# Two linear-attention and two gated-MLP layers on one core: attention output token-major, k^T v in PSUM, shared weight slots, and a written order for every engine

## The chip, the core and the metric

The kernel runs on one core of a Trainium2 chip. The metric is the time on the device in microseconds (us); each kernel is run several times and the median is quoted. The kernel before was run again beside every set of experiments; its medians there lay between 1913.2 and 1914.6 us, so medians of different sets can be compared to about 0.1%.

The engines, as these kernels use them, are PE (matrix products), DVE (vector work), ACT (functions of one input), POOL (further vector work) and SP (issues loads and stores). Matrix products are written to PSUM, which this kernel uses as eight banks of 128x512 f32; the other tiles lie in SBUF. Each engine has its own queue of instructions, and one engine can wait for another's result: PE's waits in the changed kernel add to 89 us. DVE and POOL take their instructions in queue order.

## The reference, cut to what matters

```python
# S = 2048 tokens, D = 1024, H = 32 heads of 32, F = 3584; all bf16
def A(x, wqkv, wo):                       # x is layer-normalized
    q, k, v = (x @ wqkv) split into heads
    phi = lambda t: where(t > 0, t + 1, exp(t)) + 1e-6
    kv  = phi(k)^T v          # per head, 32 x 32, summed over all tokens
    z   = sum of phi(k) over tokens
    o   = (phi(q) kv) / (phi(q) . z + 1e-6)
    return o @ wo
def B(x, w_gate, w_up, w_down):           # x is layer-normalized
    return ((x @ w_gate) * (x @ w_up)) @ w_down
x = x + A(ln(x)); x = x + B(ln(x)); x = x + A(ln(x)); x = x + B(ln(x))
```

## The kernel before

X stays on the chip as 16 tiles of 128 tokens. Tiles are normalized, transposed on PE (`xnT`), and used in groups of 512 tokens. The parts that the change and the argument touch, with cuts marked `# ...`:

```python
def phi_from_psum(ps, dst, work):            # two ACT passes, one DVE, one POOL
    m = work.tile([P, NB], F32, tag="phi_m")
    nc.scalar.activation(out=m[:], in_=ps, func=ACT.Exp)
    r = work.tile([P, NB], F32, tag="phi_r")
    nc.scalar.activation(out=r[:], in_=ps, func=ACT.Relu)
    nc.vector.tensor_scalar(out=m[:], in0=m[:], scalar1=1.0, scalar2=1e-6, op0=ALU.min, op1=ALU.add)
    nc.gpsimd.tensor_tensor(out=dst, in0=m[:], in1=r[:], op=ALU.add)

# k^T v of one 128-token tile; v carries 128 columns of ones beside its 128 columns
for c2 in range(KD // 2):
    kp = psum.tile([P, 2, 2 * P], F32, tag="aux")
    for j in range(2):
        c = c2 * 2 + j
        nc.tensor.matmul(out=kp[:, j, :], lhsT=pk[:, c * P:(c + 1) * P], rhs=v[:, c, :], start=True, stop=True)
    # ... first tile: copy
    nc.vector.tensor_tensor(out=acc[:, c2 * 2:c2 * 2 + 2, :], in0=acc[:, c2 * 2:c2 * 2 + 2, :], in1=kp[:], op=ALU.add)

# attention output of 512 tokens, channel-major: every denominator is repeated over 32 rows
for c in range(KD):
    # ... nps = numerator matmul, dps = denominator matmul, both 128x512
    den = work.tile([P, NB], F32, tag="den")
    nc.scalar.activation(out=den[:], in_=dps[:], func=ACT.Identity, bias=eps6[:], scale=1.0)
    nc.vector.reciprocal(out=den[:], in_=den[:])
    nc.vector.tensor_tensor(out=oT[:, c, :], in0=nps[:], in1=den[:], op=ALU.mult)
# ... then oT @ wo, added to X
```

The program text names no order of execution across its parts. A scheduler takes the instructions, knows their dependences, and decides in which order each engine gets them; for instance it lets the first gate matmuls of layer B run inside the output stage of layer A.

## Time and profile before

| | |
|---|---|
| time | 1913.93 us (1913.43 to 1914.03, 3 runs) |
| PE busy | 1756 us, 92% of the span |
| large matmuls (128x512) that any version needs | 7424 |
| DVE / ACT / POOL busy | 801 / 410 / 167 us |

From the page, the span in 40 slices: tenths busy of PE and DVE, and the PE clock that was granted, in tenths.

```profile
PE   5999756799999999999999995677999999999999
...
DVE  7554699941221222222254448999211211211211
...
PEclk9999877899999999999999997788999999999999
```

Twice PE falls to 5 to 7 tenths while DVE rises to 9: these are the output stages of the two attention layers. The windows view gives this stage by stage (each line: the stretch, its length, then busy time of each engine, clock, DMA share and GB/s):

```profile
core 0: us, PE busy (x) PEld busy (x) DVE busy (x) ACT busy (x) POOL busy (x), PEclk, DMA share, GB/s
0.00:18.50 18.50, 0.30 (x4) 0.30 (x5) 11.30 (x31) 2.13 (x5) 2.49 (x8) 1.00 0.95 332
18.50:223.00 204.50, 193.19 (x1021) 96.50 (x1020) 115.97 (x216) 103.82 (x169) 81.15 (x64) 0.99 0.10 32
223.00:386.00 163.00, 102.68 (x366) 38.66 (x366) 157.81 (x148) 30.00 (x46) 0.00 (x0) 0.76 0.12 39
386.00:975.00 589.00, 586.98 (x2822) 269.81 (x2821) 141.84 (x256) 85.05 (x149) 1.53 (x2) 1.00 0.32 102
```

The lines are the start, QKV (the products with wqkv), the attention output, and layer B. In the third, DVE is busy 158 of 163 us. What it does there is in the groups view (instructions of one line of the program: busy us, mean ns of one, idle time before them):

```profile
L194 DVE RECIPROCAL den<-den 128x512 f32<-128x512 f32 x64 | 211.0, 3325 | 3.4 <-ACT den L193 3.4
```

64 reciprocals of 3.3 us: 6.5 ns per element, and 31 of 32 results are copies. Layer B, in contrast, is at PE's floor. Its timeline (start, duration, engine, instructions) shows units of eight matmuls that start 1.73 us apart, 216 ns for a matmul:

```profile
450.74 1.89 PE L231 MATMUL gp<-xnT,wg 128*128 128x512 bf16 x8
452.46 1.89 PE L235 MATMUL up<-xnT,wu 128*128 128x512 bf16 x8
```

### The profile page before, as it was taken

Reading aid. Unit: us, or ns where it says so; the run is one execution under the profiler, and the core shown is the slowest. Engines: PE = TensorE matmul, PEld = TensorE weight load, DVE = VectorE, ACT = ScalarE, POOL = GpSimd, SP = SyncE. Lnnn points to the kernel's source line nnn. Section 1 sums busy time; section 2 is a strip of 40 time slices with the busy share of each in tenths; the row PEclk is TensorE's granted clock in tenths of the full one; section 3 lists DMA queues with packets and bytes.
Section 4 is the critical chain, followed back from the end, with each engine's and each line's share of the span. In section 5 each row is a group of like instructions: output and inputs, shape, how many; then the busy total and the mean of one; then the engine's idle time right before and its main releaser. Section 6 shows DMA issues by size and latency. Waiting matters only on the chain.

```text
span 1916.1 us, 19920 instructions
## 1 busy us (share of the span) xinstructions
PE 1756.1 (92%) x8320; PEld 802.8 (42%) x8320; DVE 801.0 (42%) x1159; ACT 410.4 (21%) x689; POOL 166.8 (9%) x138
## 2 busy tenths in 40 slices
PE   5999756799999999999999995677999999999999
PEld 2444322344444444444444442233444444444444
DVE  7554699941221222222254448999211211211211
ACT  5544211211111111111134442121111111110110
POOL 2344200000000000000034441000000000000000
PEclk9999877899999999999999997788999999999999
DMA  7000210084135125122050004001840540450410
GB/s 263 1 1 1 77 56 0 1 274 143 45 97 167 45 88 164 57 88 88 1 176 1 1 1 132 0 1 52 277 135 20 163 145 22 139 169 23 132 44 23
DMA packets 145882, 158.57 MB, mean 83 GB/s; under 512 B 3456, under 2 KB 134528, under 8 KB 145792
## 3 DMA queue, kind: packets, MB, share of 16 engines
q1 hardware_dynamic: 136000, 139.47, 22.7%
q10 hardware_dynamic: 9792, 17.83, 2.7%
q8 instruction: 65, 1.06, 0.2%
q14 instruction: 25, 0.20, 0.0%
HBM read 153.09 MB, written 4.19 MB: 82 GB/s over the span
## 4 chain that ended last, share of the span: by engine, by line
PE 79%; DVE 11%; DMA 3%; issue 3%; ACT 2%; POOL 0%; ACTq 0%; POOLq 0%; DVEq 0%
PE ps L249 20%; PE gp L231 19%; PE up L235 19%; PE ps L154 11%; DVE den L194 7%; PE ps L143 4%; PE ps L201 3%; PE kp L168 1%; DVE oT L195 1%; DMA wg<-in_B_w_gate_dram 1%; DMA wd<-in_B_w_down_dram 1%; DVE X L204 1%; PE pt L101 1%; ACT xnT L102 1%; DMA X<-in_A_x_dram 1%
## 5 line engine op out<-in xcount | busy, mean ns | idle before, releaser
L231 PE MATMUL gp<-xnT,wg 128*128 128x512 bf16 x1792 | 426.0, 381 | 1.2 <-ACT gs L238 1.2
L235 PE MATMUL up<-xnT,wu 128*128 128x512 bf16 x1792 | 424.0, 379 | 0.6 <-DVE hT L239 0.6
L239 DVE TENSOR_TENSOR hT<-gs,up 128x512 bf16<-128x512 f32 x224 | 153.6, 686 | 581.5 <-PE up L235 559.9
L249 PE MATMUL ps<-wd,hT 128*128 128x512 bf16 x1792 | 391.5, 379 | 0.0
L238 ACT COPY gs<-gp 128x512 f32<-128x512 f32 x224 | 131.0, 585 | 760.6 <-PE gp L231 718.7
L231 PEld LDWEIGHTS <-wg 128*128 128x128 bf16 x1792 | 176.1, 98 | 215.6 <-issue 6.1
L235 PEld LDWEIGHTS <-wu 128*128 128x128 bf16 x1792 | 175.1, 98 | 212.6 <-issue 1.2
L249 PEld LDWEIGHTS <-hT 128*128 128x128 bf16 x1792 | 174.4, 98 | 206.5
L154 PE MATMUL ps<-wqkv,xnT 128*128 128x512 bf16 x1024 | 235.7, 381 | 1.4 <-ACT r L115 1.4
L194 DVE RECIPROCAL den<-den 128x512 f32<-128x512 f32 x64 | 211.0, 3325 | 3.4 <-ACT den L193 3.4
L201 PE MATMUL ps<-wo,oT 128*128 128x512 bf16 x512 | 150.8, 445 | 37.9 <-DVE oT L195 26.7
L252 DVE TENSOR_TENSOR X<-X,ps 128x512 bf16<-128x512 bf16 x64 | 44.0, 688 | 320.7 <-PE ps L249 320.7
L154 PEld LDWEIGHTS <-xnT 128*128 128x128 bf16 x1024 | 100.3, 98 | 107.9 <-issue 2.5
L116 DVE TENSOR_SCALAR m<-m 128x512 f32<-128x512 f32 x128 | 73.1, 571 | 125.4 <-ACT m L113 125.4
L143 PE MATMUL ps<-xnT,wqkv 128*128 128x512 bf16 x512 | 112.1, 379 | 3.8 <-ACT xnT L102 3.3
L113 ACT ACTIVATE m<-ps 128x512 f32<-128x512 f32 x128 | 76.5, 597 | 178.7 <-PE ps L154 140.3
L201 PEld LDWEIGHTS <-oT 128*128 128x128 bf16 x512 | 55.2, 109 | 131.4 <-issue 55.7
L102 ACT COPY xnT<-pt 128x1024 bf16<-128x1024 bf16 x64 | 61.1, 1021 | 225.3 <-PE pt L101 223.0
L187 PE MATMUL nps<-pqT,KVm 128*128 128x512 bf16 x64 | 33.1, 517 | 80.8 <-DVE oT L195 73.2
L117 POOL TENSOR_TENSOR pk<-m,r 128x512 bf16<-128x512 f32 x64 | 81.0, 1266 | 132.0 <-ACT r L115 129.4
L193 ACT ACTIVATE den<-dps,eps_77 128x512 f32<-128x512 f32 x64 | 43.7, 686 | 225.5 <-DVE oT L195 189.1
L117 POOL TENSOR_TENSOR pqT<-m,r 128x512 bf16<-128x512 f32 x64 | 81.2, 1269 | 109.7 <-ACT r L115 99.6
(42 smaller groups left out, 707.8 us busy)
## 6 DMA issues: line engine op xcount, KB each, us to landing
wg<-in_B_w_gate_dram SPq DMA_DIRECT2D x56, 1024.0 KB, 5.4
wu<-in_B_w_up_dram SPq DMA_DIRECT2D x56, 1024.0 KB, 7.4
wd<-in_B_w_down_dram ACTq DMA_DIRECT2D x56, 256.0 KB, 5.6
wqkv<-in_A_wqkv_dram SPq DMA_DIRECT2D x12, 1024.0 KB, 12.0
wo<-in_A_wo_dram SPq DMA_DIRECT2D x4, 1024.0 KB, 12.9
out_dram<-X SPq DMA_DIRECT2D x16, 256.0 KB, 2.0
X<-in_A_x_dram ACTq DMA_DIRECT2D x12, 256.0 KB, 6.1
X<-in_A_x_dram SPq DMA_DIRECT2D x4, 256.0 KB, 4.5
```

Of the source, the lines that this page charges most:

```text
L102: nc.scalar.copy(out=xnT[:, :, tl * P:(tl + 1) * P], in_=pt[:])
L113: nc.scalar.activation(out=m[:], in_=ps, func=ACT.Exp)
L117: nc.gpsimd.tensor_tensor(out=dst, in0=m[:], in1=r[:], op=ALU.add)
L143: nc.tensor.matmul(out=ps[:], lhsT=wqkv[:, k, c * P:(c + 1) * P], rhs=xnT[:, k, :], start=(k == 0), stop=(k == KD - 1))
L154: nc.tensor.matmul(out=ps[:], lhsT=xnT[:, k, tl * P:(tl + 1) * P], rhs=wqkv[:, k, D + n * NB:D + (n + 1) * NB], start=(k == 0), stop=(k == ...
L194: nc.vector.reciprocal(out=den[:], in_=den[:])
L201: nc.tensor.matmul(out=ps[:], lhsT=oT[:, c, tl * P:(tl + 1) * P], rhs=wo[:, c, n * NB:(n + 1) * NB], start=(c == 0), stop=(c == KD - 1))
L231: nc.tensor.matmul(out=gp[:], lhsT=wg[:, k, j * P:(j + 1) * P], rhs=xnT[:, k, :], start=(k == 0), stop=(k == KD - 1))
L235: nc.tensor.matmul(out=up[:], lhsT=wu[:, k, j * P:(j + 1) * P], rhs=xnT[:, k, :], start=(k == 0), stop=(k == KD - 1))
L238: nc.scalar.copy(out=gs[:], in_=gp[:])
L239: nc.vector.tensor_tensor(out=hT[:, f, :], in0=gs[:], in1=up[:], op=ALU.mult)
L249: nc.tensor.matmul(out=ps[:], lhsT=hT[:, f, tl * P:(tl + 1) * P], rhs=wd[:, f, n * NB:(n + 1) * NB], start=(f == 0), stop=(f == KF - 1))
```

## The change: its intent, and the diff

The intent was to take the wide reciprocals away and, with an order written by hand for every engine, to have PE never wait. The whole kernel was rewritten; its parts are:

1. Attention output token-major. KV carries four extra columns per 128 channels, one denominator for each head, so a tile needs 32 reciprocals per token and not 1024. The result must then be transposed on PE.
2. k^T v stays in three PSUM banks over all 16 tiles; 132 columns, not 256; no DVE adds. That leaves one bank for transposes instead of two.
3. phi: one ACT pass, min and add on POOL, a max on DVE that reads PSUM.
4. rstd (the layernorm's 1/sqrt of variance) as a power on POOL instead of ACT's square root and DVE's reciprocal.
5. Weights, `hT` and attention's intermediates share the same SBUF slots; SP alone issues the loads.
6. The scheduler is switched off (`manual_schedule`). Each engine gets its instructions in the order of the program text, which a helper `weave` interleaves.

```diff
+def weave(main, fill, first, step):
+    out, fill = [], list(fill)
+    for i, u in enumerate(main):
+        out.append(u)
+        if fill and i >= first and (i - first) % step == 0:
+            out.append(fill.pop(0))
+    return out + fill
 ...
+    ctx.enter_context(tc.manual_schedule())
 ...
+    def phi(ps, dst):
+        e = work.tile([P, NB], F32, tag="e", name="e")
+        nc.scalar.activation(out=e[:], in_=ps[:], func=ACT.Exp)
+        nc.gpsimd.tensor_scalar(out=e[:], in0=e[:], scalar1=1.0, scalar2=1e-6, op0=ALU.min, op1=ALU.add)
+        nc.vector.scalar_tensor_tensor(out=dst, in0=ps[:], scalar=1.0 + 1e-6, in1=e[:], op0=ALU.add, op1=ALU.max)
 ...
+    def o_unit(t):            # one tile: three PSUM banks of 3, 3 and 2 chunks of 132 columns
+        ...
+                den = small.tile([P, n, HC], F32, tag=f"den{n}", name="den")
+                nc.vector.tensor_scalar(out=den[:], in0=view[:, :, P:ZW], scalar1=1e-6, scalar2=None, op0=ALU.add)
+                nc.vector.reciprocal(out=den[:], in_=den[:])
+                nc.vector.tensor_tensor(out=onat[tl]..., in0=view[:, :, 0:P]..., in1=den[:]...to_broadcast([P, n, HC, 32]), op=ALU.mult)
 ...
+            ln_stats(0)
+            ln_stats(1)
+            do([apply_unit(0), tx(0, 0), stats_unit(2), k_unit(0, 0), apply_unit(1), tx(1, 0), stats_unit(3),
+                k_unit(1, 0), apply_unit(2), tx(2, 0), k_unit(2, 0), apply_unit(3), tx(3, 0), k_unit(3, 0)])
 ...
+        do(weave(kv_group(2), next_ln(3), 0, 1))
 ...
+        def out_group(g):
+            return [u for t in range(g * TPG, (g + 1) * TPG)
+                    for u in (out_unit(t, 0), out_unit(t, 1), stats_unit(t))]
+        do(weave(out_group(0), o_group(1) + to_group(1), 0, 1))
```

A `k_unit` is eight matmuls and a phi; `apply_unit` normalizes a tile on DVE; `tx` transposes it; `stats_unit` takes a tile's mean and variance on DVE and its rstd on POOL; `o_unit` and `to_unit` make and transpose a tile of the attention output.

## The prediction

> **What bounds it now.** PE is costed by start-to-start: in layer B's timeline eight 128x512 matmuls take 1.73 us, 216 ns each[...]. Busy time by stretch (windows view):
> - 0-18.5 us: hardly any PE work; rstd waits on ACT until 15.5 us behind twelve X loads. First real matmul: 23.6 us.
> - QKV, 18.5-223 and 975-1165: PE 94-98% busy.
> - Attention and output, 223-386 and 1165-1327: DVE 97%, PE 63% (some of it B's), clock 0.75. The bound is RECIPROCAL 128x512, 3.3 us x64 = 211 us, also in the chain of waits (7%).
> - B, 386-975 and 1327-1912: PE 100%, clock 1.00; at its floor.
>
> **What changes.** 7424 large matmuls stay: x 0.216 = 1603 us.
> - Removed: the wide reciprocals and their ACT copies; 128 numerator/denominator matmuls of 512 columns (28 us); 120 accumulate adds (75 us DVE); one of two ACT passes of phi (76 us); 17 table loads; loads and rstd on ACT.
> - Added: 256 token-major matmuls of 132 columns, 256 transposes. Transposes in layer B cost about 54 ns each (25 us windows hold 140 instead of 116 matmuls); so about 57 ns for 132 columns (estimate). All small matmuls together: about 72 us.
> - Moved: phi's min/add to POOL[...], its last op to DVE (0.69 us); both under the 1.73 us unit. rstd becomes a POOL power.
>
> PE floor: 1675 us.
>
> **Above it (estimates).**
> - Start, +17 us: one queue brings X then K weights; first K unit at 10-12 us, then four tiles each wait for transpose and ACT copy (1.02 us)[...].
> - Output stage, +12 us per A layer: an o unit costs DVE about 2.2 us (three den adds, three 12-element reciprocals of 0.15, three multiplies of 0.35-0.48), plus add 0.61 and stats 1.4 per tile. Where o and output units alternate, DVE needs 3.5 us per 2.2 us of PE: with three aux banks PE waits 1.3 us, three times in each of three groups.
> - Layer boundaries +8 us; tail and latencies +7 us.
>
> Of the gain, 140-150 us is in the attention stages, 10 at the start, 20 in QKV.
>
> **Prediction: 1730 us, range 1708 to 1768.** Faster by over 2%: 0.96; within: 0.03; slower: 0.01.
>
> **What would show each step.**
> - DVE busy falls from 801 to 560-600 us; RECIPROCAL 128x12 near 0.2 us.
> - PE clock near 1.00 except the start and perhaps o/output stretches (above 0.9).
> - A(0) from first matmul to first gate matmul falls from 365 to about 275 us; each B layer stays at 585 +- 5 us.
> - The waits list's largest PE entries: o matmul <- DVE (aux buffer), first K <- ACT copy; together 30-50 us of PE idleness.
> - If o-stage waits are near zero, I overstated DVE; then about 1705.
>
> **What would make it wrong.** POOL: its power or 128x512 op may be several times slower; over 1.7 us it would bound every Q unit (+0.5 us per phi is +60 us). Strict order on DVE: phi behind a waiting op blocks PE through four mm banks. Late weights: B's down weights load only once A's output weights are free, and gate/up loads queue behind these 7 MB; I expect 22 us against 41 us of slack.

The clock at the start: the trace of the kernel before has it at 1.00 there, from 18.5 to 50 us; in the changed kernel it was 0.50 from 20 to 40. The sum came to 1675 + 17 + 24 + 8 + 7 = 1731 us and was put as 1730. That POOL's part of phi would stay under the 1.73 us unit was the estimate; the nearest op measured on POOL was the two-input add, 1.27 us. The 17, 8 and 7 us are estimates too. What an o unit and the late weights cost was estimated from records of the kernel before: for the o unit, a 128x1 reciprocal of 0.15 us, 128x128 products 0.20 us apart and a 128x512 product followed after 0.60 us; for the late weights, 7.3 MB at the 332 GB/s of its start, 22 us.

## The result, and the profile after

The changed kernel takes 1808.21 us (median of 4 runs, 1806.58 to 1810.64), before 1913.98 us. The ratio is 0.9444 (95% interval 0.9431 to 0.9458). Ratios in this text are not quite the ratio of the medians. It is clearly faster, but by 106 us and not by 184, and above the predicted range (1708 to 1768).

The three rows of the page again:

```profile
PE   4889987999999999999989999789999999999999
...
DVE  2333368422211221122122225872211111111111
...
PEclk6999998999999999999999999899999999999999
```

The deep dips are gone, but PE now stands below 9 tenths in five of the first seven slices, and the clock is low in the first. In the groups view POOL has a new costly group, and the wide reciprocal has become a small one:

```profile
L197 POOL TENSOR_SCALAR e<-e 128x512 f32<-128x512 f32 x128 | 245.8, 1920 | 143.4 <-ACT e L196 136.4
...
L266 DVE RECIPROCAL den<-den 128x12 f32<-128x12 f32 x64 | 14.6, 228 | 2.2
```

The reciprocals cost what was expected (0.23 us). The POOL half of phi takes 1.92 us, more than the 1.27 us of the two-input add that POOL did in the kernel before, and more than the 1.73 us of the matmul unit that feeds it. By stage:

```profile
0.00:43.00 43.00, 17.95 (x64) 7.50 (x66) 9.50 (x19) 7.33 (x9) 10.94 (x31) 0.71 0.89 293
43.00:212.00 169.00, 152.67 (x852) 75.50 (x867) 56.89 (x97) 58.40 (x92) 99.62 (x71) 0.99 0.08 24
212.00:337.00 125.00, 105.04 (x627) 52.94 (x637) 91.55 (x239) 27.79 (x34) 39.28 (x45) 0.92 0.07 20
337.00:929.00 592.00, 585.34 (x2794) 270.85 (x2848) 130.90 (x213) 86.77 (x133) 13.34 (x32) 1.00 0.33 109
```

In the first 43 us PE is busy 18 and no other engine for even a third of the time. (DMA works at 0.89, but it loads ahead: only the first K unit waited for a load, 2.8 us.) In the second stretch no engine but PE is above 60%. Who made PE wait is in the waits view, here of PE alone (total us, times, longest; the four largest entries):

```profile
PE pt L172 <- DVE xn L165: 32.9, 17, 6.9
PE aux L261 <- DVE H L267: 27.8, 46, 1.3
PE ps L206 <- DVE H L198: 8.3, 4, 3.3
PE pt L172 <- ACT H L173: 6.9, 6, 1.2
```

All PE entries together are 89 us. `pt` is the PSUM bank of the transposes, `aux` the three banks of the o units, `ps` the four banks of the large matmuls. The first entry is transposes that wait for the normalized tile; the second, o units that wait for a bank.

The timeline of the start shows how the first comes about. One round of four:

```profile
20.29 3.60 PE L206 MATMUL ps<-W_74,xT_70 128*128 128x512 bf16 x8 [1.10 <-ACT xT_70 L173]
...
23.93 0.60 ACT L196 ACTIVATE e<-ps 128x512 f32<-128x512 f32 x1 [3.69 <-PE ps L206]
24.61 1.94 POOL L197 TENSOR_SCALAR e<-e 128x512 f32<-128x512 f32 x1 [4.11 <-ACT e L196]
26.59 0.69 DVE L198 SCALAR_TENSOR_TENSOR H<-ps,e 128x512 bf16<-128x512 f32 x1 [7.05 <-POOL e L197]
27.19 0.54 DVE L165 TENSOR_SCALAR xn<-X,mv,rstd 128x1024 bf16<-128x1024 bf16 x1
...
27.79 1.03 PE L172 MATMUL pt<-ident,xn 128*128 128x128 bf16 x8 [3.90 <-DVE xn L165]
28.86 1.01 ACT L173 COPY xT_70<-pt 128x1024 bf16<-128x1024 bf16 x1 [4.34 <-PE pt L172]
...
29.93 3.60 PE L206 MATMUL ps<-W_74,xT_70 128*128 128x512 bf16 x8 [1.10 <-ACT xT_70 L173]
```

The normalize step at 27.19 needs nothing from the phi at 26.59: its rstd was ready at 9.2 us. It is merely behind it in DVE's queue, because the text has `k_unit(1, 0)` ahead of `apply_unit(2)`. So each tile waits for exp, the POOL op and the max of the tile before it, and a round is 9.6 us. The clock is low in these rounds too: eight matmuls take 3.60 us, not 1.89, and the granted clock is 0.50 from 20 to 40 us, with gaps of 3.9 us ahead of the transposes. How long a gap must be for that is not shown; shorter gaps go with a low clock as well: in the first output stage it was 0.50 at 250.1-256.8, 277.4-280.7 and 301.3-308.0 us, and no gap between matmuls there was over 1.5 us.

In QKV, POOL's queue and DVE's queue hold each other. The timeline around a PE wait of 3.26 us:

```profile
129.34 0.69 DVE L198 SCALAR_TENSOR_TENSOR H<-ps,e 128x512 bf16<-128x512 f32 x1 [1.30 <-POOL e L197]
...
129.95 1.28 DVE L151 BATCH_NORM_STATS2 st<-X 128x6 f32<-128x512 bf16 x2
...
131.56 0.23 POOL L155 TENSOR_SCALAR ve<-mv 128x1 f32<-128x1 f32 x1 [2.25 <-DVE mv L153]
...
132.53 1.93 POOL L197 TENSOR_SCALAR e<-e 128x512 f32<-128x512 f32 x1
...
135.23 1.89 PE L206 MATMUL ps<-W_75,xT_72 128*128 128x512 bf16 x8 [3.26 <-DVE H L198]
```

The POOL op at 132.53 had its input (an exp that ended at 126.9 us); it stood behind the 0.23 us op of a layernorm, which waited for statistics on DVE, which stood behind a phi, which had waited for POOL.

To see how much is lost where, I take the starts of the matmul records and count what lies beyond 216 ns for 512 columns and 56 to 58 ns for 128 and 132 (in the changed kernel eight transposes start at 149.24 us, eight 132-column matmuls at 149.69 and the next unit at 150.16). Over all matmuls that the kernel issues these nominal times add to 1675 us, the predicted floor. Of the 133 us above it, about 34 lie before 43 us, 26 between 43 and 250 us, 20 and 22 in the two output stages, 13 in the second QKV and the boundary before it, and 5 in layer B; the rest is tail and spells of low clock. (After 43 us, starts that are just twice the nominal apart are left out of these numbers, since they can be a missing record as well as a halved clock.)

### The profile page after: what moved, and what is told of

It reads as the page before. It is cut to its first block, busy times and chain, and to the rows that moved or that the text cites. A ratio compares the mean times of both kernels' runs of the same rounds, so it can differ in the third digit from the quotient of the medians.

```text
span 1808.9 us, 20106 instructions
## 1 busy us (share of the span) xinstructions
PE 1707.1 (94%) x8535; PEld 804.7 (44%) x8704; DVE 527.6 (29%) x1030; ACT 341.7 (19%) x514; POOL 300.2 (17%) x280
## 4 chain that ended last, share of the span: by engine, by line
PE 83%; POOL 8%; DVE 6%; ACT 1%; issue 1%; DMA 0%; another core or an unknown queue 0%; SPq 0%; ACTq 0%
PE ps L302 43%; PE aux L314 21%; POOL e L197 8%; PE ps L206 5%; PE ps L288 5%; PE ps L216 5%; PE pt L172 2%; DVE H L267 2%; PE ps L248 1%; DVE st L151 1%; DVE X L280 1%; DVE den L266 1%; PE aux L231 1%; DVE H L198 1%; ACT e L196 1%
## 5 line engine op out<-in xcount | busy, mean ns | idle before, releaser
L306 DVE TENSOR_TENSOR H<-gs,ps 128x512 bf16<-128x512 f32 x224 | 154.0, 687 | 613.7 <-PE ps L302 610.9
L197 POOL TENSOR_SCALAR e<-e 128x512 f32<-128x512 f32 x128 | 245.8, 1920 | 143.4 <-ACT e L196 136.4
L305 ACT COPY gs<-ps 128x512 f32<-128x512 f32 x224 | 131.2, 585 | 731.4 <-PE ps L302 705.6
L314 PEld LDWEIGHTS <-H 128*128 128x128 bf16 x1792 | 174.2, 98 | 207.3
L280 DVE TENSOR_TENSOR X<-X,aux 128x512 bf16<-128x512 bf16 x64 | 44.0, 688 | 328.2 <-PE aux L314 312.2
L196 ACT ACTIVATE e<-ps 128x512 f32<-128x512 f32 x128 | 76.4, 597 | 179.9 <-PE ps L206 93.6
L198 DVE SCALAR_TENSOR_TENSOR H<-ps,e 128x512 bf16<-128x512 f32 x64 | 44.3, 692 | 193.4 <-POOL e L197 193.4
L302 PEld LDWEIGHTS <-W_75 128*128 128x128 bf16 x640 | 62.5, 98 | 75.7
L302 PEld LDWEIGHTS <-W_74 128*128 128x128 bf16 x640 | 62.4, 98 | 74.9
L302 PEld LDWEIGHTS <-W_77 128*128 128x128 bf16 x576 | 56.2, 98 | 68.1
L302 PEld LDWEIGHTS <-xT_73 128*128 128x128 bf16 x576 | 56.2, 98 | 68.1
L302 PEld LDWEIGHTS <-xT_72 128*128 128x128 bf16 x576 | 56.1, 98 | 67.1
L302 PEld LDWEIGHTS <-W_76 128*128 128x128 bf16 x576 | 56.0, 98 | 66.4
L151 DVE BATCH_NORM_STATS2 st<-X 128x6 f32<-128x512 bf16 x128 | 81.7, 680 | 3.5 <-DMA X<-in_A_x_dram 3.5
L302 PE MATMUL ps<-xT_71,W_75 128*128 128x512 bf16 x317 | 75.4, 379 | 0.3
L302 PE MATMUL ps<-xT_70,W_75 128*128 128x512 bf16 x318 | 75.5, 379 | 0.2
L288 PEld LDWEIGHTS <-H 128*128 128x128 bf16 x512 | 50.8, 103 | 55.9 <-issue 10.1
L302 PE MATMUL ps<-xT_70,xT_72 128*128 128x512 bf16 x316 | 75.4, 379 | 0.2
L302 PE MATMUL ps<-xT_70,xT_73 128*128 128x512 bf16 x312 | 74.8, 379 | 0.4
L302 PE MATMUL ps<-xT_71,W_76 128*128 128x512 bf16 x314 | 75.0, 379 | 0.3
L302 PE MATMUL ps<-xT_70,W_74 128*128 128x512 bf16 x310 | 74.8, 379 | 0.4
```

The lines of the kernel that those rows point to most:

```text
L151: nc.vector.bn_stats(out=st[:, c, :], in_=X[:, t, c * NB:(c + 1) * NB])
L196: nc.scalar.activation(out=e[:], in_=ps[:], func=ACT.Exp)
L197: nc.gpsimd.tensor_scalar(out=e[:], in0=e[:], scalar1=1.0, scalar2=1e-6, op0=ALU.min, op1=ALU.add)
L198: nc.vector.scalar_tensor_tensor(out=dst, in0=ps[:], scalar=1.0 + 1e-6, in1=e[:], op0=ALU.add, op1=ALU.max)
L280: nc.vector.tensor_tensor(out=X[:, t, n * NB:(n + 1) * NB], in0=X[:, t, n * NB:(n + 1) * NB], in1=ps[:], op=ALU.add)
L288: nc.tensor.matmul(out=ps[:], lhsT=oT[(t // TPG) % 2][:, c, tl * P:(tl + 1) * P], rhs=wo[n][:, c, :], start=(c == 0), stop=(c == KD - 1))
```

## The experiments

Theory: nothing that the change computes is too slow; the written order makes PE wait, because long chains stand ahead of independent work in the in-order queues of DVE and POOL. Rivals: the POOL op is a bound by its rate; DVE's total in the output stage is; loads and the low clock (0.50 from 20 to 40 us; the expectations call it cold) set the start; the shared slots keep layer B out of the output stage of layer A. All thirteen kernels below gave correct results; unless something else is said, each has four runs, and its edit is against the changed kernel.

### e1_start and e1b_start: the order of the start

```diff
-            do([apply_unit(0), tx(0, 0), stats_unit(2), k_unit(0, 0), apply_unit(1), tx(1, 0), stats_unit(3),
-                k_unit(1, 0), apply_unit(2), tx(2, 0), k_unit(2, 0), apply_unit(3), tx(3, 0), k_unit(3, 0)])
+            do([apply_unit(0), tx(0, 0), stats_unit(2), apply_unit(1), tx(1, 0), stats_unit(3),
+                apply_unit(2), tx(2, 0), k_unit(0, 0), apply_unit(3), tx(3, 0),
+                k_unit(1, 0), k_unit(2, 0), k_unit(3, 0)])
```

> Only the first four tiles are reordered: the four normalize steps and three of the four transposes stand ahead of the first K unit, so that no normalize step stands behind a phi on DVE's queue. In the changed kernel the four rounds start 9.6 us apart and end at 43 us. Theory (in-order DVE queue: normalize of tile t+1 waits for exp, the 1.9 us POOL op and phi of tile t): the four K units now follow one another, the fourth ends at 20 to 27 us, and the whole takes about 1790 us (18 less). Rival (loads of X and weights, or the cold PE clock, set the pace): rounds stay 7 to 10 us apart, the whole stays within 5 us of 1808.

Measured: 1792.57 us (ratio 0.937), 16 us less than the changed kernel. The one normalize step that I had left behind a phi made PE wait 3.9 us again, and the 56 matmuls from 19.77 us took 14.72 us, 263 ns each in place of 216. In e1b_start it too stands ahead of `k_unit(0, 0)`:

> As e1_start, with the fourth normalize step also ahead of the first K unit. In e1_start it alone was left behind a phi, and PE waited 3.9 us for it at 18.9 us. Theory (DVE order behind phi): that wait goes too, another 4 to 6 us off e1_start, 1786 to 1789 us in all. Rival (the rest of the start is the cold clock): the same as e1_start, 1792.

Measured: 1788.66 us (ratio 0.9343), another 3.9 us. K units follow one another from 14.0 us on. The order of DVE's queue explains 20 us at the start, part of it through the clock: the loads are as before, and 63 matmuls from 14.03 us take 15.25 us, 242 ns each, where in the changed kernel eight take 3.60, 450 ns each. What the start still loses beyond the nominal time of its matmuls is 14 us.

### e2_phi_act and e2_pool_one_op: POOL's part of phi

```diff
-        nc.scalar.activation(out=e[:], in_=ps[:], func=ACT.Exp)
-        nc.gpsimd.tensor_scalar(out=e[:], in0=e[:], scalar1=1.0, scalar2=1e-6, op0=ALU.min, op1=ALU.add)
+        nc.scalar.activation(out=e[:], in_=ps[:], func=ACT.Relu, scale=-1.0)
+        nc.scalar.activation(out=e[:], in_=e[:], func=ACT.Exp, scale=-1.0)
```

exp(-relu(-x)) is min(exp(x), 1). The 1e-6 is left out here, and one in e4_all_b.

> Phi without POOL: exp(-relu(-x)) in two ACT passes, then the same DVE max. Theory (the POOL op of 1.92 us, longer than the 1.73 us unit and in one queue with the layernorm's power, starves PE): PE gaps in QKV of the first layer (26 us between 43 and 250 us, 28 us before) fall to under 12 us and the start shortens by 5 us or more; the whole takes 1775 to 1788 us. Rival (the QKV gaps come from the DVE order of layernorm work, not from POOL): under 10 us gained, 1798 or more. If two ACT passes (1.2 us per unit) become the limit instead, ACT shows above 80% in QKV and the time does not fall.

Measured: 1773.03 us (ratio 0.9269), 35 us less, a little more than expected. POOL is out of the chain of phi, and PE's waits for phi in QKV are gone from the waits view. From the end of the fourth K unit to the first o unit, gaps between matmuls fell from 18 to 2 us, and the fourth K unit ends 6 us earlier.

The other edit keeps the op on POOL, with one step of arithmetic:

```diff
-        nc.gpsimd.tensor_scalar(out=e[:], in0=e[:], scalar1=1.0, scalar2=1e-6, op0=ALU.min, op1=ALU.add)
+        nc.gpsimd.tensor_scalar(out=e[:], in0=e[:], scalar1=1.0, scalar2=None, op0=ALU.min)
```

> POOL keeps phi's min but drops the add of 1e-6, so its op has one arithmetic step in place of two (results differ far below bf16). If the 1.92 us comes from the second arithmetic step, the op falls to 1.0 to 1.3 us and the whole to 1780 to 1795 us; if it is a cost per element whatever the steps, the op stays at 1.8 to 1.95 us and the time at 1808.

Measured: 1791.32 us (ratio 0.9365). Neither branch was right about the op: it fell to 1.49 us, not to 1.0 to 1.3.

```profile
L197 POOL TENSOR_SCALAR e<-e 128x512 f32<-128x512 f32 x128 | 190.8, 1492 | 177.8 <-ACT e L196 177.1
```

The second step of arithmetic costs 0.43 us of the 1.92. At 1.49 us the op is under the unit's 1.73, and 17 us are gained. DVE is not what slows the op: at 24.61 us in the timeline of the start it takes 1.94 us while DVE stands idle.

### e3_stats: less DVE work in the output stage

```diff
         def out_group(g):
-            return [u for t in range(g * TPG, (g + 1) * TPG)
-                    for u in (out_unit(t, 0), out_unit(t, 1), stats_unit(t))]
+            outs = [out_unit(t, n) for t in range(g * TPG, (g + 1) * TPG) for n in range(2)]
+            if g < NG - 1:
+                return outs
+            return [u for t in range(TPG) for u in (stats_unit(t), outs[t])] + outs[TPG:]
 ...
-        do(weave(out_group(3), ln0, 0, 1))
+        do(weave(out_group(3), ln0, 2, 1))
 ...     # layer B, first group: statistics of the other twelve tiles between gate/up units
+                    if g == 0 and fb * 4 + j < 3 * TPG:
+                        main.append(stats_unit(TPG + fb * 4 + j))
```

> The layernorm statistics (1.41 us of DVE per tile) of twelve tiles move from the output stage into layer B's gate/up units, where DVE is about 20% busy; those of the first four move behind the last o unit. Theory (in the output stage DVE is the bound: 4 x 2.63 for o units + 8 x 0.62 + 4 x 1.41 = 21.2 us per group against 17.4 us of PE): per group 15.5 us of DVE is below PE's 17.4, the PE gaps of the output stages (20 and 22 us) fall to 8 to 14 each and the whole to 1785 to 1796 us. Rival (the stage waits on the latency of each o unit with its three aux banks, not on DVE's total): under 6 us gained.

Measured: 1780.04 us (ratio 0.9296), 28 us less, more than expected. From the first output matmul to the first gate matmul, each output stage fell from 94 to 81 us, and the gaps in it from 24 to 12 us (the 20 and 22 above are counted over shorter stretches). So the statistics did hold this stage up, by their share of DVE's time or by their place ahead of o units in its queue; the run does not tell these apart. The waits for the aux banks only fell from 27.8 to 20.0 us in total; that the rest is the latency of an o unit (2.67 us of DVE, by the mean times of its nine instructions), as the rival has it, is likely but not shown apart. The clock in the first output stage (about 250 us to its end) rose from 0.90 to 0.99, which adds to the gain.

### e_sched: the written order undone

```diff
-    ctx.enter_context(tc.manual_schedule())
```

> The changed kernel with one line removed, so that the scheduler orders every engine's instructions again; program text, tiles and shared slots stay. Theory (a good part of the lost time comes from the written order on the in-order queues of DVE and POOL): the start shortens and the QKV gaps shrink; the whole falls to 1765 to 1795 us. Rival (the loss is in the work itself: the POOL op, the o unit's DVE cost, shared slots that keep layer B out of the output stage): the whole stays at 1800 or more.

Measured: 1714.48 us (ratio 0.8955). This one line costs 94 us, more than I had expected of it, and nothing else in the program was altered: the POOL op still takes 1.92 us (246 us busy in all), the o unit has the same DVE work, and the shared slots are there. All waits of PE in this trace:

```profile
PE pt L171 <- POOL rstd L156: 9.8, 1, 9.8
PE ps L205 <- ACT xT L172: 4.7, 4, 1.4
PE ps L215 <- DVE H L197: 4.5, 3, 1.9
PE aux L260 <- DVE H L266: 4.3, 6, 1.3
PE ps L205 <- DVE H L197: 0.3, 1, 0.3
PE aux L230 <- ACT H L218: 0.3, 1, 0.3
```

That is 24 us in place of 89. At the start DVE now has all four normalize steps ahead of the first phi:

```profile
9.18 2.47 DVE L164 TENSOR_SCALAR xn<-X,mv,rstd 128x1024 bf16<-128x1024 bf16 x4
18.21 0.69 DVE L197 SCALAR_TENSOR_TENSOR H<-ps,e 128x512 bf16<-128x512 f32 x1 [6.57 <-POOL e L196]
```

### e4_all_b: all repairs in the written order

The edits of e1b_start, e2_phi_act and e3_stats, and three small ones: the reciprocal reads the denominators in PSUM directly, o and transpose units alternate, and the transposes at layer B's end are spread.

```diff
-                nc.vector.tensor_scalar(out=den[:], in0=view[:, :, P:ZW], scalar1=1e-6, scalar2=None, op0=ALU.add)
-                nc.vector.reciprocal(out=den[:], in_=den[:])
+                nc.vector.reciprocal(out=den[:], in_=view[:, :, P:ZW])
 ...
-        do(weave(out_group(0), o_group(1) + to_group(1), 0, 1))
+        do(weave(out_group(0), o_to(1), 0, 1))      # o, o, to, o, to, o, to, to; same for 1 and 2
 ...     # end of layer B: apply of the next tile together with the transposes of this one
-                    for t in range(gg * TPG, (gg + 1) * TPG):
-                        fill += [apply_unit(t), tx(t, gg)]
+                ts = range(TPG, 3 * TPG)
+                fill = [apply_unit(TPG)] + [(lambda t=t: (tx(t, t // TPG)(), t + 1 < 3 * TPG and ln_apply(t + 1))) for t in ts]
```

> All repairs of the fixed order together: start order, phi on ACT twice and DVE (no POOL), statistics moved, denominators inverted straight from PSUM (0.6 us less DVE per o unit; the 1e-6 is far below the sums), o and transpose units spread evenly, the transposes at the end of layer B spread. If the causes add up: 1808 less 21 (start), 27 (phi; its share of the start is already counted), 22 (output stages), 5 (boundary) is 1733; range 1728 to 1750, faster than the kernel before with the attention part alone (1767). If they overlap or a new wait appears: 1760 or more.

Measured: 1710.78 us (ratio 0.8933), 97 us less than the changed kernel and better than expected. The three tested causes alone add to 83 us (20 + 35 + 28); the other three edits were not tried apart, so how far the causes overlap is open. The repaired written order is as fast as the scheduler with the unrepaired work (1714 us), but not as fast as the scheduler with the same repairs (1696 us, next).

### e5_sched_phi and e5_sched_all: the scheduler with the repairs

The edit of e2_phi_act, and all edits of e4_all_b, each without the `manual_schedule` line.

> The changed kernel with the scheduler's order and phi without POOL. In the written order this repair of phi gained 35 us. Theory (the 1.92 us POOL op hurts only through what the written order puts behind it): with the scheduler's order it gains under 10 us, 1705 to 1714. Rival (POOL's rate is a bound of its own): 20 us or more gained, 1695 or less.

Measured: 1700.91 us (ratio 0.8888). Phi without POOL gains 13.6 us here and 35 in the written order. That is between the two expectations: most of what the POOL op cost came from order, but not all of it.

> All repairs of e4_all_b, but ordered by the scheduler and not as written. If order is the common cause, the repairs and the scheduler remove the same waits: 1695 to 1714 us, a few us below the better of the two (1711 and 1714), because the POOL op and 0.6 us of DVE per o unit are gone too. If the scheduler undoes the hand-made spreading: 1715 or more.

Measured: 1695.59 us (ratio 0.8857), the fastest version, 11.4% under the kernel before. Its page:

```profile
PE   7999999999999999999999999999999999999999
...
PEclk9999999999999999999999999999999999999999
```

All 8704 matmul records are in this trace. Their nominal times add to about 1675 us; the span is 1694.3 us, of which 9.5 are before the first matmul, and from the first matmul's start to the last's it is 1681 us. Little is left to gain but the start and the work itself. The four kernels make a square: written order 1808 us and repaired 1711, scheduler 1714 and repaired 1696. The order costs 94 us with the work as it was and 15 us with the repairs, so most of the loss needed both: the order, and the long chains that it put ahead of PE's work.

### p_attn: the first part of the change alone, on the kernel before

```diff
-                    for c in range(KD):
-                        # nps, dps: 128x512; den on ACT; reciprocal 128x512; multiply
+                    for tl in range(TPG):
+                        onat = work.tile([P, D], BF16, tag="onat")
+                        for c0 in range(0, KD, 3):
+                            # n = 3, 3, 2 matmuls of 132 columns into one bank; den (+1e-6), reciprocal
+                            # and multiply as in o_unit
+                        pt = psum.tile([P, KD, P], BF16, tag="tr")
+                        # eight transposes of onat into pt
+                        nc.scalar.copy(out=oT[:, :, tl * P:(tl + 1) * P], in_=pt[:])
```

> The kernel before with one part of the change alone: token-major attention output with denominators as extra columns (masked KV with 132 columns, 12-element reciprocals, PE transposes of the output), scheduler and everything else as before. Theory (the wide reciprocal was all that bounded this stage; the fixed order adds little to it): the stage falls from 163 to about 95 to 105 us in both layers and the whole to 1780 to 1810 us, as much as the full change gave. Rival (the gain needs the fixed order and the PSUM accumulation too): 1830 us or more.

Measured: 1766.91 us (1762.09 to 1771.66, ratio 0.9227), better than expected and 41 us better than the full change. This part alone gains 147 us. The output stage that began near 223 us ends at 309.5 us, 87 us later; in the kernel before it lasted to 389.5 us. The first gate matmul of layer B comes right after it:

```profile
309.69 1.89 PE L241 MATMUL gp<-xnT,wg 128*128 128x512 bf16 x8
```

This also bears on the rival of the shared slots. They are not shared here and layer B does not start inside the output stage; in e_sched they are shared, and the first gate matmul follows the last output matmul by the same 0.2 us (282.2 after 282.0). So the slots cost no overlap that another version had made use of, except the kernel before, whose output stage was idle enough to let it in. And e5_sched_all, which has the shared slots, lies only about 20 us above PE's floor.

### b_manual: the written order alone, on the kernel before

```diff
+    ctx.enter_context(tc.manual_schedule())
```

> The kernel before with its program text as it is, but executed in the written order. Theory (a written order costs wherever work with long chains stands ahead of independent work in one in-order queue): clearly slower than 1914, 1960 to 2100 us. Rival (only the weave of the changed kernel is at fault): within 1% of 1914.

Measured: 2171.77 us (2 runs, ratio 1.1345), even slower than expected: the text of this kernel was never meant to be an order. Its largest PE wait is 111 us, numerator matmuls waiting for the multiply of an earlier chunk.

### p_kv and p_kv2: k^T v in PSUM, on top of p_attn

```diff
-                acc = p1.tile([P, KD, 2 * P], F32, tag="acc")
+                        if t == 0:
+                            acc = [psum.tile([P, NB], F32, tag="aux", bufs=3, name="acc") for _ in range(3)]
+                        # eight matmuls of 132 columns accumulate into acc over all tiles; no DVE adds
 ...     # banks of PSUM: mm 4, tr 2, aux 2  ->  p_kv: mm 4, tr 1, aux 3;  p_kv2: mm 3, tr 2, aux 3
```

> The kernel before with two parts of the change: the token-major attention output (as in p_attn, 1767 us) and k^T v kept in PSUM over all tiles, 132 columns wide; scheduler, phi and weight loads as before. The three accumulator banks leave one bank for transposes instead of two. Estimate: 256 matmuls of 132 instead of 256 columns, 109 - 57 ns each, 13 us less on PE; the 75 us of DVE adds were off the chain: 1750 to 1758 us. If the single transpose bank costs more than that gains: 1767 or more.

Measured: 1790.59 us (ratio 0.9351), 24 us slower than p_attn; the estimate was wrong, and the other branch came true. The waits view of p_attn has this line for transposes that wait until ACT has copied an earlier tile out of the transpose bank:

```profile
PE pt L103 <- ACT xnT L104: 3.4, 11, 0.7
```

and in p_kv it has become

```profile
PE pt L103 <- ACT xnT L104: 21.6, 21, 1.9
```

This kernel transposes the four tiles of a group one after the other. With one bank each waits for the 1.01 us copy of the one before. p_kv2 gives the second bank back and takes one from the matmuls:

> p_kv with two transpose banks and three matmul banks in place of one and four. Theory (the single transpose bank makes PE wait for each ACT copy at every group boundary, 21.6 us of waits against 3.4 in p_attn): those waits fall below 6 us and the time to 1750 to 1772 us. Rival (the accumulators themselves, or the order that the scheduler makes of them, cost it): the time stays above 1780. If three matmul banks bind instead, PE waits for phi (ACT or DVE) appear in the QKV stage.

Measured: 1759.44 us (ratio 0.9189). The wait is 3.9 us, and the accumulation in PSUM now gains 7 us over p_attn by the medians, where 13 were estimated. This is uncertain by several us, since the runs of p_attn spread over 9.6 us; the two profiled executions differ by 12.5 us. The bank was the cost, not the accumulators. Three matmul banks bind little: PE's waits for phi's ACT pass are 2.6 us, after 1.0 in p_attn.

## Why the prediction was wrong, point by point

The direction was right. The time was not: 1808 us is 40 us above the upper end.

What held:

- The bound before. p_attn removes the wide reciprocal, keeps the scheduler, and gains 147 us: within the 140 to 150 that the prediction gave to the attention stages. The changed kernel itself did not get all of it.
- The PE floor of 1675 us. The nominal times of the matmuls add to it again, which only repeats the sum; but e5_sched_all takes 1681 us from its first matmul to its last.
- Layer B at 585 +- 5 us each, nearly: from its first matmul to its last the first takes 593 us (337.1 to 930.6, with the transposes at its end), which is just outside, and the second 585 (1219.8 to 1805.1). The loads of shared slots cost no visible wait.
- A 12-element reciprocal near 0.2 us: 0.23. DVE busy fell further than said, to 528 us and not 560 to 600.

The step that failed is "Above it (estimates)": 55 us were allowed for what PE loses, and 133 were lost.

| term | predicted | measured | what the runs showed |
|---|---|---|---|
| start | 17 | about 34 | the normalize step of each tile stood behind the phi of the tile before (e1b_start: 20 us; the 14 left are within the 17) |
| output stages | 2 x 12 | 20 and 22 of gaps | an o unit keeps DVE 2.67 us, not 2.2; statistics on top of it and a clock of 0.90 (e3_stats: 28 us) |
| QKV, boundaries, tail, latencies | 15 | 39 in the two QKV stretches, and 5 in B | the POOL op in one queue with the layernorm's small ops (e2_phi_act: 35 us, a part of it at the start) |

Two sentences of the prediction are at the root. The first is "both under the 1.73 us unit", of phi's parts on POOL and DVE. For POOL that was the author's estimate and not measured; the op took 1.92 us. The prediction's own warning ("+0.5 us per phi is +60 us") would make about 24 us of the 0.19 us over the unit; without POOL 35 us were gained in the written order (e2_phi_act) and 13.6 in the scheduler's (e5_sched_phi). The second is the whole treatment of the written order: the prediction named "Strict order on DVE: phi behind a waiting op blocks PE" among what could go wrong, and costed it at nothing. It was in the text of the program to be read, `k_unit(1, 0)` ahead of `apply_unit(2)`. What the order costs is measured: 94 us (e_sched), of the 133 that the time lies above PE's floor. Without them, at 1714 us, the time would have stood inside the range.

The checks that it named: A(0) from the first matmul of a projection to the first gate matmul was to fall "from 365 to about 275 us"; it fell to 326 us (10.7 to 337.1). The 365 was itself misread: the first gate matmul of the kernel before is at 370.9 us, inside the output stage, so 347 was the figure. The largest waits were to be aux banks and the first K, 30 to 50 us together; they were normalized tiles and aux banks, 89 us for all. The clock of the output stages was to be above 0.9 and was 0.92 in the third stretch, 0.90 in the output stage within it.

What stays open: how the scheduler's gain divides among the engines' queues, since the order was only switched for all of them at once; which of the three untested edits of e4_all_b gains what; and whether p_kv2 gains 7 us or the 13 that were estimated.

## What to carry to other kernels

On an in-order queue, as DVE's and POOL's are in these traces, the place of an instruction is a dependence. Before an order is written by hand, follow each queue and ask what stands ahead of every instruction that PE will need, in particular the last step of a chain over several engines; and leave the scheduler on unless a run shows that the written order beats it. Try the parts of a large rewrite one at a time: here one part alone (147 us) was worth more than all of them together (106 us), and one deleted line made the whole worth 199 us.
